# Long-run loads of q and k, one DMA transpose per batch and shared PSUM banks in an attention and channel-mix kernel

## The chip, the cores and the metric

The kernel runs on one core of one Trainium2 chip. The metric is the device time in microseconds (us) of one execution. An execution of the kernel before took 299.62 us (median of three; 299.26 to 300.0). The profile's span is about 1.7 us shorter than the measured time of the same execution. Each execution has a state: slow is one that took over 1.5% longer than the fastest run of the same kernel, the others are fast.

In this text, PE is the matmul engine (TensorE), DVE VectorE, ACT ScalarE, POOL GpSimd, and SP the engine whose queue issues most DMAs. PSUM is the memory that the matmuls write; this program uses eight banks of it, and an instruction of ACT or DVE that reads a result out of a bank is called its evacuation here.

## The reference, cut to what matters

```python
def _attn_ref(q, k, v):                       # (8 batches, 8 heads, 576 positions, 64), fp32
    scores = q @ k^T / 8
    mask_plain = (rel >= 0) & (rel < 32)                      # heads 0..3
    mask_dil   = (rel >= 0) & (rel < 128) & (rel % 4 == 0)    # heads 4..7
    attn = softmax(where(mask, scores, -1e9))
    return attn @ v

def _moe_ref(x, mu_k, mu_r, w_k, w_v, w_r):   # x (8, 576, 512): attention output, heads side by side
    xk = mu_k * x + (1 - mu_k) * x_prev       # x_prev: the position before
    xr = mu_r * x + (1 - mu_r) * x_prev
    k  = relu(xk @ w_k)                       # 512 -> 1024
    v  = k * k @ w_v                          # 1024 -> 512
    return sigmoid(xr @ w_r) * v
```

A batch goes through attention, and its output is mixed into XK and XR (the inputs of the channel mix). The channel mix works in nine tiles of 128 x 4 positions over all eight batches and needs 720 matmuls of 128 x 128 by 512 columns. I call the moment when a batch's XK is complete "that batch's input is ready".

## The kernel before

Every operation is first entered in a list with its engine, an estimated duration, its dependencies and a priority. A small planner then fixes the order on each engine by simulating that list, and the instructions are issued in that order. Each engine, and SP's queue too, then has to take its instructions in the order that was planned, also where an operation comes later than the planner assumed (in e17 below SP stands for 28 us in this way).

```python
pools = {"qk": 2, "st": 7, "v": 2, "kqd": 2, ..., "kr": 2, "K2": 2, "th": 3, "ot": 3, "cm": 4, "pa": 2}
CM = many(4, [128, 512], FP32, "CM", psp)       # channel mix: 4 PSUM banks of its own
PA = many(2, [128, 2, 512], FP32, "PA", psp)    # attention: 2 double banks
def sp_dma(xfer, fn, n=1, **kw):
    return P.op("SP", 0.06 * n, fn, xfer=xfer, **kw)   # planner: a DMA issue takes 0.06 us

def load_qk_cast(b, prio, after=()):            # batches 1..7: POOL issues DMAs that cast fp32 to fp16
    for n_, (part, i) in enumerate(((0, 1), (0, 0), (1, 1), (1, 0))):
        a, e = ((0, 96), (96, 144))[part]       # 96 and 48 partitions, runs of 4 rows (1 KB)
        ... nc.gpsimd.dma_start(out=qk_dst(bq.idx, i, 0, 8, part), in_=qk_src(i, b, 0, 8, a, e))

def pd(i, part, eng):                           # dilated heads: four DMA transposes a batch
    if b > 0:
        ... nc.sync.dma_start_transpose(out=KQD[kqd.idx][:, i, :, p0:p0 + n], in_=...)
        KDR[i, part] = sp_dma(..., tr, dep=[L[1, i, part]], use=[bq, kqd], prio=nxt(0.001))  # 10*b + ...

# channel mix: relu on ACT, square on DVE, tanh on ACT, last product on DVE
nc.scalar.activation(out=KR[kr.idx][:, g], in_=CM[pk.idx], func=AF.Relu, scale=0.5 ** 0.5)
nc.vector.tensor_tensor(out=K2[k2.idx][:, 2 * f2:2 * f2 + 2], in0=KR[kr.idx], in1=KR[kr.idx], op=ALU.mult)
nc.scalar.activation(out=TH[th.idx], in_=CM[pr.idx], func=AF.Tanh, scale=0.5)
nc.vector.scalar_tensor_tensor(out=OT[ot.idx], in0=TH[th.idx], scalar=1.0, in1=CM[pv.idx], op0=ALU.add, op1=ALU.mult)
# ... (cut: v in six windows of 512 packets of 256 B and two dilated parts, scores, softmax, mixing)
```

The softmax here doesn't subtract the row's maximum and nothing guards it: scores larger than these inputs give would overflow.

Of the kernel before, what the change touches and what calls it, by code (L numbers as in the profile page):

```python
# [22 lines left out]
class Op:  # L23
    __slots__ = ("eng", "dur", "fn", "dep", "use", "prio", "lock", "n", "start", "end", "lat", "xfer", "nsucc", "succ", "ready")


class Plan:


    def __init__(self, pools):  # L30
        self.ops = []
        self.pools = pools

    def op(self, eng, dur, fn, dep=(), use=(), prio=0.0, lock=False, lat=None, xfer=None):
        o = Op()
        o.eng, o.dur, o.fn, o.prio, o.lock = eng, dur, fn, prio, lock
        o.dep = [d for d in dep if d is not None]
        o.use = list(use)
        for b in o.use:
            b.left += 1  # L40
        o.lat = {"PE": 0.13, "ACT": 0.08, "DVE": 0.08, "POOL": 0.12, "SP": 0.0}[eng] if lat is None else lat
        o.xfer = xfer
        o.n = len(self.ops)
        o.start = o.end = None
        self.ops.append(o)
        return o

    def run(self, pe_slack=0.12):
        free = {k: [0.0] * n for k, n in self.pools.items()}
        busy = {k: [False] * n for k, n in self.pools.items()}  # L50
        turns = {k: 0 for k in self.pools}
        t_eng = {"PE": 0.0, "ACT": 0.0, "DVE": 0.0, "POOL": 0.0, "SP": 0.0}
        t_dma = 0.0
        dve_lock_end = pool_lock_end = 0.0
        for o in self.ops:
            o.nsucc = len(o.dep)
            o.succ = []
        for o in self.ops:
            for d in o.dep:
                d.succ.append(o)  # L60
        ready = {e: [] for e in t_eng}
        for o in self.ops:
            o.ready = 0.0
            if o.nsucc == 0:
                ready[o.eng].append(o)
# [3 lines left out]
        def slot(b):  # L69
            if b.idx is not None:  # L70
                return 0.0
            fr, bs = free[b.pool], busy[b.pool]
            if b.turn is not None:
                i = b.turn % len(fr)
                return None if bs[i] or turns[b.pool] != b.turn else fr[i]
            c = [fr[i] for i in range(len(fr)) if not bs[i]]
            return min(c) if c else None

        while left:
            best = None  # L80
            for e, lst in ready.items():
                te = t_eng[e]
                be = None
                for o in lst:
                    r = max(te, o.ready)
                    ok = True
                    for b in o.use:
                        s = slot(b)
                        if s is None:
                            ok = False  # L90
                            break
                        r = max(r, s)
                    if not ok:
                        continue
                    if o.lock:
                        r = max(r, pool_lock_end if e == "DVE" else dve_lock_end)
                    k = (r if r > te + 1e-9 else te, o.prio, o.n)
                    if be is None or k < be[0]:
                        be = (k, o)
                if be is not None and (best is None or be[0] < best[0]):  # L100
                    best = be
            assert best is not None, "no operation can start"
            (t, _, _), o = best
            e = o.eng
            ready[e].remove(o)
            for b in o.use:
                if b.idx is None:
                    fr, bs = free[b.pool], busy[b.pool]
                    if b.turn is not None:
                        i = b.turn % len(fr)  # L110
                        turns[b.pool] += 1
                    else:
                        i = min((j for j in range(len(fr)) if not bs[j]), key=lambda j: fr[j])
                    b.idx = i
                    bs[i] = True
            o.start = t
            t_eng[e] = t + o.dur
            o.end = t + o.dur + o.lat
            if o.lock:
                if e == "DVE":  # L120
                    dve_lock_end = t + o.dur
                else:
                    pool_lock_end = t + o.dur
            if o.xfer is not None:
                t_dma = max(t_dma, t + o.dur + 0.6) + o.xfer
                o.end = t_dma + 1.5
            for b in o.use:
                b.left -= 1
                if b.left == 0:
                    free[b.pool][b.idx] = o.end + (0.05 if e != "PE" else 0.0)  # L130
                    busy[b.pool][b.idx] = False
            for s in o.succ:
                s.nsucc -= 1
                sl = pe_slack if s.eng == "PE" and e != "PE" else 0.0
                s.ready = max(s.ready, o.end + sl if s.eng != e else (o.end if o.xfer is not None else t + o.dur))
                if s.nsucc == 0:
                    ready[s.eng].append(s)
# [18 lines left out]
def kernel(  # L156
# [18 lines left out]
    VS = 66  # L175
# [6 lines left out]
    pools = {"qk": 2, "st": 7, "v": 2, "kqd": 2, "qt": 2, "at": 3, "xs": 3, "rc": 4, "xT": 2, "dx": 1,  # L182
             "ring": NR, "kr": 2, "K2": 2, "th": 3, "ot": 3, "cm": 4, "pa": 2}
    P = Plan(pools)
# [4 lines left out]
    QA = many(2, [96, 2, 8, 256], FP16, "QA")  # L189
    QB = many(2, [112, 8, 256], FP16, "QB")  # L190
    ST = many(pools["st"], [128, 1024], FP32, "ST")
    VP = many(2, [128, 6, 4, VS], FP16, "VP")
    VD1 = many(2, [112, 4, 4, VS], FP16, "VD1_")
    VD2 = many(2, [64, 4, 4, VS], FP16, "VD2_")
    KQD = many(2, [128, 2, 8, NP], FP16, "KQD")
    QT = many(2, [128, 2, 4, NP], FP16, "QT")
    KT = many(2, [128, 2, S], FP16, "KT")
# [9 lines left out]
    TH = many(pools["th"], [128, DM], FP32, "TH")  # L207
    OT = many(pools["ot"], [128, DM], FP32, "OT")
# [3 lines left out]
    nmk = const.tile([128, 4], FP32, name="nmk")  # L212
    nmr = const.tile([128, 4], FP32, name="nmr")
# [4 lines left out]
    CM = many(4, [128, 512], FP32, "CM", psp)  # L218
    PA = many(2, [128, 2, 512], FP32, "PA", psp)

    def buf(pool, turn=None):
        return Buf(pool, turn)

# [15 lines left out]
    def setup_mp():  # L239
        nc.vector.tensor_copy(out=MP.rearrange("p (r i) -> p r i", r=4),  # L240
                              in_=M[:, 32:128].rearrange("p (i r) -> p r i", r=4))
# [3 lines left out]
    def setup_m0():  # L245
        for wl in range(2):
            nc.vector.tensor_copy(
                out=M0.rearrange("p (a w h) (r i) -> p w a h r i", a=2, w=2, r=4)[:, wl, 0, 0],
                in_=M[:, 32 * wl:32 * wl + 96].rearrange("p (i r) -> p r i", r=4))
        src = M0.rearrange("p (a w h) c -> p w a h c", a=2, w=2)  # L250
        for wl in range(2):
            for a in range(2):
                for h in range(2):
                    if a or h:
                        nc.vector.tensor_copy(out=src[:, wl, a, h], in_=src[:, wl, 0, 0])

    m0_op = P.op("DVE", 1.6, setup_m0, dep=[mask_op], prio=-8)
# [9 lines left out]
    def setup_zero():  # L267
        for t in AT:
            nc.vector.memset(t, 0.0)
        for t in XT:  # L270
            nc.vector.memset(t[:, :, :, 0:2], 0.0)

    zero_op = P.op("DVE", 1.2, setup_zero, prio=-20)

    def load_mu():
        with nc.allow_non_contiguous_dma(reason="mu"):
            nc.sync.dma_start(out=nmk, in_=moe_mu_k.rearrange("(c p) -> p c", p=128))
            nc.sync.dma_start(out=nmr, in_=moe_mu_r.rearrange("(c p) -> p c", p=128))

    def fix_mu():  # L280
        nc.vector.tensor_scalar(out=nmk, in0=nmk, scalar1=-1.0, scalar2=None, op0=ALU.add)
        nc.vector.tensor_scalar(out=nmr, in0=nmr, scalar1=-1.0, scalar2=None, op0=ALU.add)


    def cast(eng, o, i):
        {"DVE": nc.vector.tensor_copy, "POOL": nc.gpsimd.tensor_copy, "ACT": nc.scalar.copy}[eng](out=o, in_=i)  # L286

    def cast_op(eng, n, o, i, **kw):
        d = {"DVE": dve2(n), "POOL": 0.1 + 0.0009 * n, "ACT": act(n)}[eng]
        return P.op(eng, d, lambda: cast(eng, o(), i()), lock=eng != "ACT", **kw)  # L290

    def sp_dma(xfer, fn, n=1, **kw):
        return P.op("SP", 0.06 * n, fn, xfer=xfer, **kw)

    def pool_dma(xfer, fn, n=1, **kw):
        return P.op("POOL", 0.66 * n, fn, xfer=xfer, **kw)

    W = {}

    def load_w(name, dst, src, eng, prio, cprio=None):  # L300

        s = buf("st")
        shape = dst.shape

        def ld():
            t = ST[s.idx]
            if len(shape) == 3:
                t = t.rearrange("p (a n) -> p a n", a=shape[1])
            nc.sync.dma_start(out=t, in_=src)

        def st():
            t = ST[s.idx]
            return t.rearrange("p (a n) -> p a n", a=shape[1]) if len(shape) == 3 else t

        d = sp_dma(1.35, ld, use=[s], prio=prio)
        W[name] = cast_op(eng, 1024, lambda: dst, st, dep=[d], use=[s], prio=prio if cprio is None else cprio)

    qs = {0: q, 1: k}
    LD = {}

    def qk_src(i, b, h0, h1, a, e):
        return qs[i][b, h0:h1].rearrange("h (p r) d -> p h (r d)", r=4)[a:e]

    def qk_dst(slot, i, h0, h1, part):
        if part == 0:
# [549 lines left out]
```

## Time and profile before

| stretch (us) | what happens | PE busy |
|---|---|---|
| 0 to 39 | weights and batch 0 load; batch 0's input is ready at 39.1 | 17 us |
| 39 to 89 | batch 1; its input is ready only at 89.2 | 31.5 us |
| 89 to 259 | batches 2 to 7, 28.4 us each | 152 of 170 us |
| 259 to 298 | the last two tiles, with no attention left, then the last store | 34.7 us |

From the page of the kernel before: span, busy time of each engine, and the span in 40 slices of 7.5 us, each digit the busy share of a slice in tenths (PEclk is PE's granted clock in tenths).

```profile
span 298.3 us, 5959 instructions
...
PE 234.5 (79%) x2336; PEld 124.9 (42%) x2336; DVE 180.3 (60%) x355; ACT 161.6 (54%) x254; POOL 52.3 (18%) x75
...
PE   1544679922659995699899949997999899599994
...
PEclk9999979975576999599999997999999799999999
DMA  8999999999999999994752792054003102200322
```

PE is the busiest engine, but its ninth and tenth slices are nearly empty, while the DMA engines are full there. The table of stretches puts numbers on this. After the stretch it gives its length, then the busy time of each engine with the count of instructions, PE's granted clock, the mean busy share of the DMA engines (transfers in flight overlap, so it can exceed 1) and GB/s.

```profile
...
core 0: us, PE busy (x) PEld busy (x) DVE busy (x) ACT busy (x) POOL busy (x), PEclk, DMA share, GB/s
60.00:90.00 30.00, 12.85 (x192) 8.60 (x193) 15.89 (x31) 9.64 (x15) 7.15 (x9) 0.61 1.26 209
89.20:259.40 170.20, 151.68 (x1576) 79.31 (x1576) 119.88 (x238) 102.55 (x168) 27.99 (x33) 0.94 0.63 116
```

In the 30 us from 60 to 90 PE worked 12.9 us, and at a clock of 0.61. The Trainium skill ("TensorE: Matmul & The Clock Gate", Part 1) says that an idle array falls to half its clock; the trace agrees: eight matmuls of 512 columns (the product with wv, L795) took 3.55 us at 80.5 us and 1.89 to 1.90 us in the 35 other groups. From 89 to 259 us PE stood still for 18.5 us of 170.

What PE waited for, in the waits view (us in total, times, longest; KQD is the transposed q and k of the dilated heads):

```profile
...
PE CM L752 <- DVE XK L706: 18.1, 8, 4.6
PE PA L568 <- DMA KQD<-QB: 7.2, 1, 7.2
```

SP's own queue in this time, from the timeline (start, duration of the issue, instruction). L372 and L389 load v, L457 is a transpose.

```profile
...
30.07 12.92 SPq L372 DMA_DIRECT2D ST<-in_v_dram  x6
43.09 1.66 SPq L389 DMA_DIRECT2D ST<-in_v_dram  x2
44.85 1.65 SPq L372 DMA_DIRECT2D ST<-in_v_dram  x3
46.60 2.64 SPq L457 DMA_TRANSPOSE KQD<-QA  x1
49.34 4.06 SPq L372 DMA_DIRECT2D ST<-in_v_dram  x3
53.50 2.18 SPq L389 DMA_DIRECT2D ST<-in_v_dram  x1
55.78 5.47 SPq L457 DMA_TRANSPOSE KQD<-QA  x1
61.34 1.21 SPq L457 DMA_TRANSPOSE KQD<-QB  x1
...
63.41 1.21 SPq L457 DMA_TRANSPOSE KQD<-QB  x1
```

The transposes of batch 1 stand between loads of v that belong to later work. Those loads hold SP for long (six issues took 12.9 us), and the last of the four transposes is issued at 63.4 us. The scores of batch 1's dilated heads start at 70.5 us, after PE has waited 7.2 us for it. Two lines of DVE's timeline show when the inputs of batches 1 and 2 became ready (start and duration of the last addition):

```profile
...
87.80 1.36 DVE L706 TENSOR_TENSOR XK<-XK,XT 128x2304 f16<-128x2304 f16 x1
...
122.78 1.36 DVE L706 TENSOR_TENSOR XK<-XK,XT 128x2304 f16<-128x2304 f16 x1
```

### The profile page before, as it was taken

What the parts mean: (1) busy time and instruction counts of PE and PEld (TensorE: products, weight loads), DVE (VectorE), ACT (ScalarE), POOL (GpSimd) and SP (SyncE); (2) the same over time, 40 slices, a digit from 0 to 9 for tenths busy, and PEclk for the clock granted to TensorE, in tenths of its full rate; (3) what the DMA queues carried; (4) which work ended last, traced back from release to release, by engine and by line L of the source; (5) the groups of instructions that cost most, each with busy time, mean ns of one, the idle gap of its engine ahead of it and who ended that gap; (6) DMA issues with size and microseconds to landing.
All of it is one profiled execution on the core that took longest, in us unless ns stands there. A gap on an engine that the chain in (4) does not pass through costs nothing.

```text
span 298.3 us, 5959 instructions
## 1 busy us (share of the span) xinstructions
PE 234.5 (79%) x2336; PEld 124.9 (42%) x2336; DVE 180.3 (60%) x355; ACT 161.6 (54%) x254; POOL 52.3 (18%) x75
## 2 busy tenths in 40 slices
PE   1544679922659995699899949997999899599994
PEld 0433334421424554445455424453554355244441
DVE  4555653633764756796886638749767876833221
ACT  2518988423246735865775375638665672566220
POOL 2224008106113225232031401020000000000000
PEclk9999979975576999599999997999999799999999
DMA  8999999999999999994752792054003102200322
GB/s 168 203 224 365 306 221 210 161 158 201 261 226 171 220 193 248 203 193 77 168 150 41 117 249 82 0 108 115 2 2 105 37 1 73 70 0 2 91 96 94
DMA packets 76187, 41.87 MB, mean 140 GB/s; under 512 B 45440, under 2 KB 69504, under 8 KB 76160
## 3 DMA queue, kind: packets, MB, share of 16 engines
q1 hardware_dynamic: 59584, 33.24, 50.0%
q0 software_dynamic: 16576, 8.26, 22.9%
q8 instruction: 18, 0.29, 0.4%
q14 instruction: 9, 0.07, 0.1%
HBM read 36.18 MB, written 9.44 MB: 153 GB/s over the span
## 4 chain that ended last, share of the span: by engine, by line
PE 63%; DVE 17%; DMA 11%; SPq 5%; ACT 2%; issue 1%; POOL 0%; DVEq 0%; ACTq 0%; POOLq 0%
PE CM L752 24%; PE CM L795 18%; PE CM L788 9%; DVE XK L706 3%; DMA ST<-in_moe_w_k_dram 3%; DVE XK L698 3%; PE PA L433 3%; DMA out_dram<-OT 3%; DMA KQD<-QB 2%; DMA ST<-in_k_dram 2%; SPq L457 2%; DVE OT L799 2%; DVE XS L493 2%; PE PA L540 2%; PE PA L589 2%
## 5 line engine op out<-in xcount | busy, mean ns | idle before, releaser
L752 PE MATMUL CM<-XK,wk 128*128 128x512 f16 x288 | 77.8, 414 | 18.2 <-DVE XK L706 18.1
L795 PE MATMUL CM<-wv,K 128*128 128x512 f16 x288 | 69.9, 387 | 0.0
L756 ACT ACTIVATE KR<-CM 128x512 f16<-128x512 f32 x72 | 42.9, 598 | 30.6 <-PE CM L752 30.1
L799 DVE SCALAR_TENSOR_TENSOR OT<-TH,CM 128x512 f32<-128x512 f32 x36 | 24.7, 687 | 39.6 <-PE CM L795 33.2
L752 PEld LDWEIGHTS <-wk 128*128 128x128 f16 x288 | 27.2, 103 | 48.6 <-issue 25.9
L765 DVE TENSOR_TENSOR K<-KR 128x1024 f16<-128x1024 f16 x36 | 27.7, 770 | 23.6 <-ACT KR L756 23.5
L795 PEld LDWEIGHTS <-K 128*128 128x128 f16 x288 | 26.7, 99 | 30.2 <-issue 1.7
L788 PE MATMUL CM<-wr,XR 128*128 128x512 f16 x144 | 36.4, 380 | 0.0
L791 ACT ACTIVATE TH<-CM 128x512 f32<-128x512 f32 x36 | 21.4, 596 | 24.6 <-PE CM L788 21.0
L493 DVE TENSOR_TENSOR XS<-PA,RC 96x512 f16<-96x512 f32 (+2 forms) x48 | 30.9, 644 | 1.7 <-DVE RC L489 0.2
L521 ACT ACTIVATE AT<-PA 128x768 f16<-128x768 f32 x24 | 19.0, 807 | 14.4 <-PE PA L517 14.4
L702 ACT ACTIVATE XR<-DX,nmr 128x576 f16<-128x576 f16 (+2 forms) x36 | 23.2, 714 | 2.4 <-DVE DX L695 2.4
L579 DVE TENSOR_TENSOR AT<-AT,M 112x896 f16<-112x896 f16 x16 | 13.0, 815 | 15.8 <-ACT AT L573 15.8
L286 POOL CAST VP<-ST 128x768 f16<-128x768 f32 (+1 forms) x15 | 13.5, 904 | 50.5 <-DMA ST<-in_v_dram 26.2
L286 POOL CAST VD<-ST 112x1024 f16<-112x1024 f32 (+1 forms) x15 | 15.5, 1048 | 28.9 <-PE PA L589 22.2
L573 ACT ACTIVATE AT<-PA 112x896 f16<-112x896 f32 x16 | 14.4, 914 | 9.0 <-PE PA L568 8.9
L445 ACT ACTIVATE KT<-PA 128x768 f16<-128x768 f16 (+1 forms) x16 | 10.4, 652 | 15.8 <-PE PA L433 15.7
L788 PEld LDWEIGHTS <-XR 128*128 128x128 f16 x144 | 12.8, 98 | 13.4 <-issue 0.5
L433 PE MATMUL PA<-ident,QA 96*64 96x96 f16 x256 | 10.7, 241 | 8.0 <-DVE QA L286 5.5
L605 ACT ACTIVATE XT<-PA 128x448 f16<-128x448 f16 x16 | 8.7, 542 | 14.7 <-PE PA L601 14.6
L568 PE MATMUL PA<-KQD 64*112 64x112 f16 x128 | 7.1, 247 | 9.1 <-DMA KQD<-QB 7.2
L540 PE MATMUL PA<-VP,AT 128*128 128x65 f16 x192 | 10.8, 205 | 4.2 <-ACT KQD L477 2.8
(73 smaller groups left out, 259.8 us busy)
## 6 DMA issues: line engine op xcount, KB each, us to landing
ST<-in_v_dram SPq DMA_DIRECT2D x48, 128.0 KB, 6.5
ST<-in_v_dram SPq DMA_DIRECT2D x8, 448.0 KB, 6.9
QA<-in_k_dram POOLq DMA_DIRECT2D x7, 384.0 KB, 8.4
QA<-in_q_dram POOLq DMA_DIRECT2D x7, 384.0 KB, 9.4
ST<-in_v_dram SPq DMA_DIRECT2D x8, 256.0 KB, 6.8
ST<-in_moe_w_k_dram SPq DMA_DIRECT2D x4, 512.0 KB, 9.1
ST<-in_moe_w_v_dram SPq DMA_DIRECT2D x4, 512.0 KB, 10.9
out_dram<-OT SPq DMA_DIRECT2D x8, 256.0 KB, 5.3
```

What stands on the lines that cost most here:

```text
L286: {"DVE": nc.vector.tensor_copy, "POOL": nc.gpsimd.tensor_copy, "ACT": nc.scalar.copy}[eng](out=o, in_=i)
L433: nc.tensor.transpose(out=t[64 * e:64 * e + 64, hp * 4 + r], in_=src_qk(i, part, 2 * hp + e, 64 * r), identity=idn(i, part), tile_position ...
L493: nc.vector.tensor_tensor(out=XS[xs.idx][0:n, 0:g].rearrange("p w (h d) -> p w h d", h=4), in0=fin(po)[0:n, :, :, 0:64], in1=RC[rc.idx][0: ...
L521: nc.scalar.activation(out=AT[at.idx][:, :, 0:96].rearrange("p (a g) c -> p a g c", a=2), in_=PA[ps.idx][:, :, 0:384].rearrange("p a (g c) ...
L702: nc.scalar.activation(out=XR[:, c, :, a:a + n], in_=DX[0][:, c, :, o:o + n], func=AF.Copy, scale=nmr[:, c:c + 1])
L752: nc.tensor.matmul(out=o, lhsT=wk[:, c, f * 128:f * 128 + 128], rhs=XK[:, c, :, a0:a0 + 128], start=(c == 0), stop=(c == 3))
L756: nc.scalar.activation(out=KR[kr.idx][:, g], in_=CM[pk.idx], func=AF.Relu, scale=0.5 ** 0.5)
L765: nc.vector.tensor_tensor(out=K2[k2.idx][:, 2 * f2:2 * f2 + 2], in0=KR[kr.idx], in1=KR[kr.idx], op=ALU.mult)
L788: nc.tensor.matmul(out=CM[pr.idx], lhsT=XR[:, c, r, a:a + 128], rhs=wr[:, c], start=(c == 0), stop=(c == 3))
L791: nc.scalar.activation(out=TH[th.idx], in_=CM[pr.idx], func=AF.Tanh, scale=0.5)
L795: nc.tensor.matmul(out=CM[pv.idx], lhsT=K2[k2.idx][:, f, 128 * r:128 * r + 128], rhs=wv[:, f], start=(f == 0), stop=(f == NF - 1))
L799: nc.vector.scalar_tensor_tensor(out=OT[ot.idx], in0=TH[th.idx], scalar=1.0, in1=CM[pv.idx], op0=ALU.add, op1=ALU.mult)
```

## The change

Its intent: load q and k of the plain heads in runs of 2304 B over all 128 partitions and of the dilated heads in rows of 1 KB, without a casting DMA; cast on POOL (batch 0 and 1: on any free engine); turn the dilated q and k of a batch in one DMA transpose that is planned right after their load; let attention and channel mix share PSUM banks (from batch 1 on they overlap in banks 4 and 5), for which all eight banks become four tiles PA of two banks each; and let the planner choose between DVE and ACT for some copies and scalings. The planner itself got other costs.

```diff
-pools = {..., "cm": 4, "pa": 2}
-CM = many(4, [128, 512], FP32, "CM", psp)         # before: each bank of the channel mix is a tile of its own
-PA = many(2, [128, 2, 512], FP32, "PA", psp)
+PA = many(4, [128, 2, 512], FP32, "PA", psp)      # after: two banks in each tile
+P = Plan(pools, {"pa": OPTIONS["pa"], "p1": OPTIONS["p1"], "cm": OPTIONS["cm"], ...})
+OPTIONS = dict(..., split=1, pa=[(0, 1), (2, 3), (4, 5)], p1=[(0,), (1,), (2,), (3,)],
+               cm=[(4,), (5,), (6,), (7,)], ..., p=0, v=0, xe=0, sk=('DVE','ACT'), sr=('DVE','ACT'),
+               ep='P', ed='P', er='P', ev='P', ew='P', st=5, b1=dict(ep='*', ed='*', ..., ew='P'))
-    return P.op("SP", 0.06 * n, fn, xfer=xfer, **kw)
+    return P.op("SP", t or 0.47 * n, fn, xfer=xfer, **kw)
+def load_plain_qk(b, prio, cprio, engs):
+    for n_, (i, t) in enumerate(((1, k), (0, q))):
+        src = t[b, 0:4].rearrange("(g e) (x y) d -> (e x) g (y d)", g=2, x=64)     # runs of 9 rows
+        LD[b]["p", i] = piece(1.65, 1152, ..., src, lambda i=i: QP[bq.idx][:, i], engs[n_], ...)
         if b > 0:
             def tr():
-                nc.sync.dma_start_transpose(out=KQD[kqd.idx][:, i, :, p0:p0 + n], in_=...)
-            KDR[i, part] = sp_dma(..., tr, dep=[L[1, i, part]], use=[bq, kqd], prio=nxt(0.001))
+                nc.sync.dma_start_transpose(out=KQD[...].rearrange("p a (g x) -> p (a g) x", x=128),
+                                            in_=QD[bq.idx].rearrange("p a g x -> p (a g x)"))
+            KDR.append(sp_dma(..., tr, t=OPT["ttr"], dep=list(parts_), use=[bq, kqd], prio=-90 + 10 * b + 0.15))
+    W["wr"] = P.op("POOL", 0.7, lambda: nc.gpsimd.dma_start(out=wr, in_=wrr), ...)   # wr, wv: casting DMA
# ... (cut: v of the plain heads in two DMAs of the same 256 B runs, masks, planner internals)
```

## The prediction

> **What bounds the kernel now.** The page gives PE 234.5 of 298.3 us busy. The table of stretches shows where the other 64 us lie: PE was busy 7.2 of the first 20 us, 10.4 of 20 to 40, and only 12.9 of 60 to 90 (granted clock 0.61 there), i.e. 49 of the first 90 us. From 122.8 to 259.5 us PE was busy 122.7 of 136.7 us (five batches, 27.3 us each), and the last 34.7 us are PE alone. So before about 120 us DMA feeds too slowly (mean DMA share 1.03 to 1.34); after it PE is the limit with 10% gaps.
>
> The stall at 60 to 90 us is read in the timeline: batch 1's four transposes of the dilated q and k were issued at 46.6, 55.8, 61.3 and 63.4 us, one queue entry held SP for 5.5 us, and they stood between v loads of which each 512-packet window held SP about 1.1 us. The scores of the dilated heads waited 7.2 us for the last one (waits view), batch 1's channel-mix input was ready at 89.2 us and batch 2's at 124 us.
>
> **What the change removes, adds, moves.**
> - DMA packets: q/k of a batch go from 2304 cast packets of 1 KB (queue 0: 22.9% of 16 engines over 16,576 packets, about 66 ns each) to 512 long runs plus 1152 runs of 1 KB without a cast. v keeps its 256 B packets. Four transposes a batch become one, planned early. Estimate: DMA time per batch falls by only 10 to 20%, but the queue order and SP's blocking improve more.
> - POOL: casts grow. One costs about 1.04 us per 1024 columns (lines view); q, k and v of a batch are about 8200 columns, so about 8.5 us a batch, some 65 us in all, against 29 us now. The Trainium skill (SBUF — State Buffer, "SBUF: two separate sides") says that the pair of ports shared by GpSimd and VectorE is locked for a whole instruction. The trace agrees: one mask multiply on DVE (L579, median 0.62 us) took 3.48 us beside POOL casts at 72 us. This eats a part of the gain.
> - PSUM: attention gets three double banks and shares eight; this trims the 10% gaps, by perhaps 2 to 6 us.
> - PE work stays nearly equal: 720 large matmuls, floor 0.216 us each (0.865 us per four in the chain), 156 us; the attention's about 45 us.
>
> **On the critical path.** Estimate: batch 1's channel-mix input comes at about 60 instead of 89 us and batch 2's at about 88 instead of 124. Then five periods of about 26.5 us to the last batch, its first channel-mix matmul at about 221 instead of 259.5, and 35 to 37 us to the end: about 257 us.
>
> **Prediction: 257 us**, eight times in ten between 243 and 275. Faster by over 2%: 0.94; within 2%: 0.04; slower: 0.02.
>
> **What would show it.** Right: PE over 85% of the span; first channel-mix matmul of batch 1 before 65 us; one transpose issue per batch; last batch's tail still about 35 us; packets 10 to 20% fewer; POOL busy 60 us or more. Wrong: the same stall at 60 to 90 us, with SP still blocked by v loads, or periods over 28 us with PE waiting for DVE while POOL casts.
>
> **What would make it wrong.** DVE stretched by POOL's casts in the steady state (slower, 270 and more); a first stage that is much shorter because long runs move faster (245 or less); a single transpose that lands late because it now needs all casts of a batch.

## The result and the profile after

The changed kernel took 276.77 us (median of four; fast runs 275.05, 276.28 and 277.26, one slow run of 279.64; the median of the fast ones alone is 276.28), against 299.81 us for the kernel before. The ratio of the two is 0.92 (interval 0.913 to 0.927). Ratios here are the mean time of one kernel's fast runs over that of the other's of the same rounds, so not quite the ratio of the medians that are quoted. So the kernel is 8% faster, but the prediction of 257 us (243 to 275) is 20 us too low and its range just misses.

The same lines of the page, kernel after (slices of 6.8 us):

```profile
span 273.3 us, 6031 instructions
...
PE 226.9 (83%) x2388; PEld 122.5 (45%) x2388; DVE 185.8 (68%) x377; ACT 155.0 (57%) x260; POOL 69.3 (25%) x85
...
PE   1564986899998599899998879988886889999992
...
PEclk9995599599999989999999999999999999999999
DMA  7999999989999999999998995940021012110331
```

The hole at 60 to 90 us is gone. The same table of stretches, the second one again from batch 1's input to batch 7's:

```profile
...
60.00:90.00 30.00, 28.19 (x316) 14.99 (x316) 22.35 (x42) 18.23 (x33) 12.90 (x14) 1.00 1.06 234
63.40:231.40 168.00, 146.80 (x1618) 78.78 (x1617) 127.87 (x260) 102.13 (x176) 52.25 (x52) 0.99 0.72 174
```

From 60 to 90 us PE now works 28.2 us in place of 12.9, at full clock. But from batch 1's input to batch 7's the kernel needs 168.0 us where it needed 170.2, and PE's idle time there is 21.2 us (168.0 less 146.8) where it was 18.5. For the five periods from batch 2's to batch 7's input alone, the kernel before and then the kernel after:

```profile
...
124.14:259.43 135.29, 122.63 (x1226) 62.91 (x1226) 97.43 (x199) 81.94 (x136) 15.40 (x17) 0.96 0.44 92
...
94.50:231.42 136.92, 120.04 (x1314) 64.27 (x1314) 103.50 (x215) 83.08 (x143) 39.63 (x40) 0.99 0.65 161
```

SP's queue and the two inputs, in the timeline:

```profile
...
31.55 2.65 SPq L366 DMA_DIRECT2D ST<-in_v_dram  x2
38.67 5.88 SPq L494 DMA_TRANSPOSE KQD<-QD  x1
44.60 0.56 SPq L366 DMA_DIRECT2D ST<-in_k_dram  x1
```

```profile
...
62.65 0.76 DVE L724 TENSOR_TENSOR XK<-XK,XT 128x1152 f16<-128x1152 f16 x1
...
93.03 1.47 DVE L724 TENSOR_TENSOR XK<-XK,XT 128x1152 f16<-128x1152 f16 x1
```

Batch 1's transpose (L494) is issued at 38.7 us, before any load of batch 2, and batch 1's input is ready at 63.4 in place of 89.2 us. That is 26 us, slightly more than the whole gain. What PE waits for has changed too, in the waits view:

```profile
...
PE PA L780 <- ACT KR L784: 5.4, 13, 0.8
PE PA L780 <- DVE XK L724: 5.0, 3, 2.6
PE PA L830 <- ACT TH L826: 2.9, 5, 1.2
...
PE PA L780 <- ACT TH L826: 2.4, 2, 1.7
...
PE PA L823 <- DVE OT L834: 0.8, 2, 0.4
...
PE PA L596 <- DMA KQD<-QD: 0.3, 1, 0.3
```

The view's largest line, 6.0 us for batch 0's q and k (QP) in the first 20 us, is left out; the kernel before waits 5.5 us there. PE no longer waits long for XK (it did for 18.1 us). New are waits for the relu (KR), the tanh (TH) and the last product (OT), which free PSUM banks: in the whole run they sum to 13.6 us, all such lines of the view added. The kernel before has none.

### The profile page after: what moved, and what is told of

Its sections match the earlier page's. It is cut to its first block, busy times and chain, and to the rows that moved or that the text cites. A ratio compares the mean times of both kernels' runs of the same rounds, so it can differ in the third digit from the quotient of the medians.

```text
span 273.3 us, 6031 instructions
## 1 busy us (share of the span) xinstructions
PE 226.9 (83%) x2388; PEld 122.5 (45%) x2388; DVE 185.8 (68%) x377; ACT 155.0 (57%) x260; POOL 69.3 (25%) x85
## 2 busy tenths in 40 slices
DMA packets 68732, 48.49 MB, mean 177 GB/s; under 512 B 43096, under 2 KB 59488, under 8 KB 68704
## 4 chain that ended last, share of the span: by engine, by line
PE 53%; DVE 16%; ACT 13%; DMA 11%; issue 6%; SPq 1%; POOL 0%; ACTq 0%; DVEq 0%; POOLq 0%
PE PA L830 18%; PE PA L780 17%; PE PA L823 9%; DMA ST<-in_q_dram 5%; ACT KR L784 4%; DVE OT L834 3%; DMA KQD<-QD 3%; ACT TH L826 3%; DMA ST<-in_moe_w_k_dram 2%; PE PA L481 2%; DVE K L794 2%; DVE XS L524 2%; DVE XT L338 1%; DVE AT L558 1%; ACT XT L334 1%
## 5 line engine op out<-in xcount | busy, mean ns | idle before, releaser
L780 PE MATMUL PA<-XK,wk 128*128 128x512 f16 x288 | 72.4, 397 | 13.2 <-ACT KR L784 5.4
L830 PE MATMUL PA<-wv,K 128*128 128x512 f16 x288 | 69.7, 386 | 3.6 <-ACT TH L826 2.9
L784 ACT ACTIVATE KR<-PA 128x512 f16<-128x512 f32 x72 | 40.5, 596 | 40.2 <-PE PA L780 29.2
L834 DVE SCALAR_TENSOR_TENSOR OT<-TH,PA 128x512 f32<-128x512 f32 x36 | 24.7, 685 | 36.1 <-ACT TH L826 15.7
L823 PE MATMUL PA<-wr,XR 128*128 128x512 f16 x144 | 36.8, 379 | 2.6 <-DVE OT L834 0.8
L826 ACT ACTIVATE TH<-PA 128x512 f32<-128x512 f32 x36 | 21.3, 598 | 30.2 <-PE PA L830 21.2
L336 POOL CAST QD<-ST 128x1024 f16<-128x1024 f32 (+1 forms) x19 | 17.5, 930 | 30.8 <-DMA ST<-in_k_dram 14.8
L336 POOL CAST QP<-ST 128x1152 f16<-128x1152 f32 x12 | 15.1, 1262 | 16.0 <-DMA ST<-in_k_dram 8.9
L724 DVE TENSOR_TENSOR XK<-XK,XT 128x1152 f16<-128x1152 f16 (+2 forms) x18 | 14.0, 787 | 4.2 <-ACT XK L718 3.8
L718 ACT ACTIVATE XR<-DX,nm 128x576 f16<-128x576 f16 (+2 forms) x21 | 15.0, 736 | 0.0
```

What stands on the lines that cost most here:

```text
L336: nc.gpsimd.tensor_copy(out=o, in_=i)
L780: nc.tensor.matmul(out=o, lhsT=wk[:, c, f * 128:f * 128 + 128], rhs=XK[:, c, :, a0:a0 + 128], start=(c == 0), stop=(c == 3))
L784: nc.scalar.activation(out=KR[kr.idx][:, g0:g0 + G], in_=view(), func=AF.Relu, scale=0.5 ** 0.5)
L823: nc.tensor.matmul(out=view(pr)[:, g], lhsT=XR[:, c, rr[g], a:a + 128], rhs=wr[:, c], start=(c == 0), stop=(c == 3))
L826: nc.scalar.activation(out=TH[th.idx][:, 0:m], in_=view(pr), func=AF.Tanh, scale=0.5)
L830: nc.tensor.matmul(out=view(pv)[:, g], lhsT=K2[k2.idx][:, f, 128 * rr[g]:128 * rr[g] + 128], rhs=wv[:, f], start=(f == 0), stop=(f == NF - 1))
```

## The experiments

Labels beginning with e are runs; those on the changed kernel are compared with its 276.8 us, those on the kernel before with 299.8 us. "Input ready" is read from DVE's timeline.

### 1. Three rival causes of the missing 20 us: banks, DMA packets, POOL's casts

**e1**: give the channel mix its four banks back.

```diff
-pa=[(0, 1), (2, 3), (4, 5)]
+pa=[(0, 1), (2, 3)]
```

> The changed kernel with the attention's third double bank (4,5) taken away, so the channel mix has banks 4 to 7 to itself as before the change. Theory P (sharing the banks makes PE wait for evacuations): PE's waits for ACT KR, ACT TH and DVE OT in the steady state, 12.5 us between batch 1's and batch 7's input, fall under 4 us, and the time falls by 6 to 12 us to 265 to 271 us. Rival (the sharing pays or does not matter): within 1% of 276.8 us or slower, and waits for XK or for attention results take the place.

Measured: 275.13 us, ratio to the kernel before 0.921 (0.912 to 0.930), so the same as with shared banks. PE's waits for KR, TH and OT halved, from 13.6 to 6.8 us, but waits on the attention (AT, the weights of the softmax, and XT, the attention output turned) came in their place, as these lines of its waits view show; the path from batch 1's to batch 7's input took 169.9 us.

```profile
...
PE PA L569 <- DVE AT L558: 3.4, 6, 0.9
PE PA L780 <- ACT KR L784: 2.9, 7, 0.5
PE PA L547 <- DVE XT L338: 2.2, 1, 2.2
```

Between batch 1's and batch 7's input these waits fell from 12.5 to 6.6 us, not under 4, and the time fits the rival. Sharing banks 4 and 5 neither earned the 2 to 6 us that the prediction gave it nor cost anything. e1 leaves two banks in each tile; part 2 comes back to this.

**e2**: the same bytes of v in long runs (wrong result).

```diff
-in_=bass.AP(v.tensor, a.offset, [[D, 128], [96 * D, 23], [1, D]])
+in_=bass.AP(v.tensor, v[b, 0].offset, [[23 * D, 128], [D, 23], [1, D]])
```

> Wrong result on purpose: the plain heads' v is fetched in 128 long runs of 5.9 KB a batch in place of 2944 runs of 256 B; bytes, instructions and their order stay the same. Theory D (loads still set the pace after the change): batch 1's input comes 3 us earlier or more, later periods shorten, 265 us or less. Rival (the pace is set on PE, ACT and DVE): within 1.5%, 273 to 278 us, with the DMA share falling to about 0.8 in 60 to 150 us.

Measured: 276.09 us, batch 1's input at 64.1 us; packets fell from 68,732 to 46,204, the DMA share over the first 180 us only from 1.01 to 0.94, and the time did not move. The Trainium skill ("DMA: Bandwidth & Descriptors", Why small descriptors are slow) warns of a fixed cost per packet; here 2,800 packets of 256 B less per batch did not shorten the run, since the loads are not what the steady state waits for.

**e3**: from batch 2 on, POOL copies 8 columns of each row group only (wrong result).

```diff
+    if CUT and engs == ("POOL",):       # CUT is set from batch 2 on
+        return P.op(engs[0], costs(n, engs)[engs[0]], lambda: copy(engs[0], cut(o()), cut(i())), **kw)
```

> Wrong result on purpose: from batch 2 on every cast on POOL copies 8 columns of each row group in place of all; order and waits stay the same. Theory C (POOL's casts lengthen DVE through the shared ports and so the periods): 260 to 268 us, and DVE busy falls by 5 us or more. Rival (the casts lie beside the critical path): within 1.5% of 276.8 us, DVE busy falls by 2 to 4 us only.

Measured: 273.81 us (three fast runs of 271.4 to 274.6 us, one slow), ratio 0.914 (0.900 to 0.927), not to be told from the changed kernel's 0.92 (0.913 to 0.927). The busy line of its page:

```profile
...
PE 224.9 (82%) x2388; PEld 122.0 (45%) x2388; DVE 174.2 (64%) x377; ACT 155.1 (57%) x260; POOL 28.7 (11%) x85
```

With POOL at 28.7 in place of 69.3 us, DVE fell from 185.8 to 174.2 us although it did the same work. So the casts do lengthen DVE's instructions, by 11.6 us in all, in agreement with the Trainium skill ("SBUF — State Buffer", SBUF: two separate sides: the pair of ports shared by GpSimd and VectorE is locked for a whole instruction). But most of this lies beside the critical path: the mean of the fast runs is 3 us lower, and even that is within the intervals.

### 2. Which engines hold PE in the steady state

**e5**: from the fourth tile on, relu, square, tanh and last product work on 64 of 512 columns (wrong result; the order of all engines stays).

```diff
+Z = 512 if i < 3 else 64
-nc.scalar.activation(out=KR[kr.idx][:, g0:g0 + G], in_=view(), func=AF.Relu, ...)
+nc.scalar.activation(out=KR[kr.idx][:, g0:g0 + G, 0:Z], in_=view()[:, :, 0:Z], func=AF.Relu, ...)
# the square, the tanh and the last product likewise
```

> Wrong result on purpose: from the fourth channel-mix tile on, relu, square, tanh and the last product work on 64 of 512 columns; matmuls, order and waits stay. Theory E (PE's 21 us of gaps between batch 1's and batch 7's input come from in-order ACT and DVE holding PSUM banks and attention work): PE idle there falls below 12 us and the time to 262 us or less. Rival W (PE's own work, more than the prediction summed, fills the periods): within 2% of 276.8 us.

Measured: 262.96 us. The stretch from batch 1's to batch 7's input, in the table of stretches:

```profile
...
63.90:219.30 155.40, 144.84 (x1618) 77.84 (x1617) 114.62 (x260) 85.82 (x176) 51.19 (x52) 0.99 0.78 188
```

It is 155.4 us, and PE idles for 10.6 us of it in place of 21.2. From batch 3's input on its idle time is 0.7 to 1.0 us a batch, where the changed kernel has 2.7 to 4.0. So theory E holds in its direction, and 262.96 us is just above its forecast of 262: what ACT and DVE do for the channel mix sets PE's gaps. 263 us is also close to what was predicted for the real kernel.

**e6**: the 480 large matmuls of tiles 4 to 9 with 256 columns; the evacuations read those 256 twice, so keep their size (wrong result).

```diff
+Z = 128 if i < 3 else 64
-nc.tensor.matmul(out=o, lhsT=wk[...], rhs=XK[:, c, :, a0:a0 + 128], ...)
+nc.tensor.matmul(out=o[...4 * Z columns...], lhsT=wk[...], rhs=XK[:, c, :, a0:a0 + Z], ...)
# XR @ wr and K @ wv likewise
```

> Wrong result on purpose: from the fourth tile on the 480 large matmuls have 256 columns in place of 512, about 51 us less PE work at 0.107 us each; evacuations keep their size. If PE's work alone fills the periods (W), the time falls by 40 us or more to 236 us or less. If ACT, DVE and their order set the pace (E), it falls by under 20 us, to 257 us or more.

Measured: 244.95 us, 32 us less for 51 us less PE work: between the two forecasts. PE idles more (33.0 us on that stretch, which took 151.0 us). PE's work is a large part of the pace and ACT and DVE are close behind it; no single engine is "the" limit.

**e10**: as e5, but on DVE only (square and last product; relu and tanh full).

```diff
-nc.vector.tensor_tensor(out=K2[...][:, 2 * f2:2 * f2 + 2], in0=KR[kr.idx], in1=KR[kr.idx], op=ALU.mult)
+nc.vector.tensor_tensor(out=K2[...][:, 2 * f2:2 * f2 + 2, 0:Z], in0=KR[kr.idx][:, :, 0:Z], ...)
# the last product likewise
```

> Wrong result on purpose: the changed kernel with only DVE's square and last product on 64 of 512 columns from the fourth tile on, ACT's relu and tanh full. If DVE is what holds PE, most of the 14 us of the run with all four short are kept, 267 us or less; if ACT is, 272 us or more.

Measured: 270.66 us, between the two forecasts. DVE's part gives 6 of the 14 us; the other 8 come only when ACT's part is shortened too. (By the ratios to the kernel before in the same rounds, 0.907 and 0.878 against 0.92, it is some 4 of 13 us.)

**e9**: e5's edit on the kernel before (wrong result).

```diff
-nc.scalar.activation(out=KR[kr.idx][:, g], in_=CM[pk.idx], func=AF.Relu, ...)
+nc.scalar.activation(out=KR[kr.idx][:, g, 0:Z], in_=CM[pk.idx][:, 0:Z], func=AF.Relu, ...)
# the square, the tanh and the last product likewise
```

> Wrong result on purpose: the kernel before with the same shortening of relu, square, tanh and last product as in the run on the changed kernel that gave 263 us. If the evacuations bind only after the change (a limit that the change uncovered), the kernel before loses under 2%, 294 us or more. If they bound before too, it falls by 10 to 15 us, to 285 to 290 us.

Measured: fast runs of 294.1 to 297.7 us, ratio 0.989 (0.980 to 0.998), about 3 us; one execution, the profiled one, was slow (401 us, clock 0.60), so its trace is not used. The same shortening is worth 14 us after the change and 3 us before it. The evacuations hardly bound before; after the change they do.

A count made from both traces shows the same from the other side. I paired each relu, tanh and last product with the matmuls that it reads, in the program's order, over the stretch from batch 1's to batch 7's input, and took the time from the end of those matmuls to its start:

| mean lag behind its matmuls, us | kernel before | kernel after |
|---|---|---|
| relu (KR) | 0.11 | 0.53 |
| tanh (TH) | 0.10 | 0.67 |
| last product (OT) | 0.54 | 0.56 |

In the kernel before ACT nearly always stood ready. In the kernel after, a bank stays taken for 1.12 us after a relu's matmuls in place of 0.71. ACT is no busier in this stretch (102.1 us of 168.0 against 102.6 of 170.2), so it is its order and what it waits for, not its load, that differ.

What it waits for can be read in the timeline. Eight matmuls, four for each of two relus, and the two relus, in the kernel before:

```profile
...
97.78 1.89 PE L752 MATMUL CM<-XK,wk 128*128 128x512 f16 x8
...
98.84 0.60 ACT L756 ACTIVATE KR<-CM 128x512 f16<-128x512 f32 x1
...
99.77 0.60 ACT L756 ACTIVATE KR<-CM 128x512 f16<-128x512 f32 x1 [0.33 <-PE CM L752]
```

and in the kernel after:

```profile
...
126.02 1.89 PE L780 MATMUL PA<-XK,wk 128*128 128x512 f16 x8 [0.35 <-ACT KR L784]
...
127.94 1.08 ACT L784 ACTIVATE KR<-PA 128x512 f16<-128x512 f32 x2 [1.17 <-PE PA L780]
```

Before, the first relu starts at 98.84 us, when half of the matmuls are done (the brackets give the idle time before and who ended it). After, both start only when all eight are done, at 127.9 us: the trace has no signal (no semaphore update, for which ACT could wait) at the end of the first relu's own four matmuls. In the stretch this is so for 13 of 48 relus and 5 of 23 tanhs, which start 1.1 and 1.8 us behind their own matmuls (the others 0.31 and 0.35 us); in the kernel before, and in e8, for none.

The plan of the changed kernel was printed with the bank of each operation. In all 18 cases matmuls for the other bank of the same two-bank tile are planned between the evacuation and its own matmuls; in the 51 cases where none are, no signal is missing. The other way round, of PE's 13.6 us of waits for KR, TH and OT, 11.5 us (23 of 27) are, as the profile puts them down, for the evacuation of the other bank of the tile that PE is about to write. So this program orders its work by tile, and two banks in one tile wait for each other. What that costs in time no run tests, since every variant of the changed kernel has the same tiles; e1 lost half of these waits, and its time stayed the same within the intervals.

### 3. Which part of the change brought the gain

**e7**: the transpose as four, at the same place.

```diff
+for g0, g1 in ((0, 5), (5, 9), (9, 14), (14, 18)):
+    nc.sync.dma_start_transpose(out=KQD[...][:, g0:g1], in_=QD[...][:, 128 * g0:128 * g1])
```

> The single DMA transpose of a batch's dilated q and k is issued as four transposes of 4 or 5 blocks, at the same place in the same order. If one transpose in place of four is what took the 60 to 90 us stall away, batch 1's input comes 5 us later or more and the time rises by over 2%. If the place in the queue and the plain loads did it, within 1% of 276.8 us.

Measured: 277.02 us over all four runs, two of them slow; the two fast ones took 272.79 and 276.56 us, ratio 0.917 (0.907 to 0.926); batch 1's input at 63.7 us in a profile of a slow execution. One transpose or four makes no difference that these runs show.

**e16**: the transpose with its old priority, all else as changed.

```diff
-dep=list(parts_), use=[bq, kqd], prio=-90 + 10 * b + 0.15)
+dep=list(parts_), use=[bq, kqd], prio=nxt(0.001))
```

> The DMA transpose gets its old priority, so that on the SP queue it stands behind the next batch's loads. If its place removed the stall, batch 1's input comes at 75 us or later and the time is 288 us or more; if the plain loads and the packets did, batch 1's input stays below 68 us and the time within 2% of 276.8 us.

Measured: 300.14 us (the kernel before, in its two fast runs of the same rounds: 295.31 and 299.5): the whole gain is gone. SP's queue in the timeline, PE's largest wait, and the stretch from 60 to 90 us:

```profile
...
63.03 0.59 SPq L421 DMA_DIRECT2D SV<-in_v_dram  x1
63.67 5.64 SPq L418 DMA_DIRECT2D SV<-in_v_dram  x1
69.35 6.70 SPq L494 DMA_TRANSPOSE KQD<-QD  x2
```

```profile
...
PE PA L596 <- DMA KQD<-QD: 9.9, 2, 7.9
```

```profile
...
60.00:90.00 30.00, 14.09 (x244) 10.68 (x245) 15.16 (x30) 10.83 (x17) 14.78 (x15) 0.55 1.07 240
```

The transpose of batch 1 (with that of batch 2) is issued at 69.4 us behind the loads of batches 2 and 3, batch 1's input is ready at 90.5 us, and PE works 14.1 of the 30 us, at a clock of 0.55. The planner reordered PE, DVE and ACT too, so this is not a change of SP's order alone, but the chain is visible step by step.

**e4**: from batch 2 on, q and k of the plain heads and their v by casting DMA again.

```diff
-p=0, v=0, xe=0
+p=1, v=1, xe=0
```

> One part undone: from batch 2 on q and k of the plain heads and their v are cast by DMA again, from POOL's queue, in place of a plain load and a POOL cast. If the gain came from taking the casts out of DMA, the time rises to 285 us or more and waits for loaded data come back; if it came from the order of the transposes and the queue, the time stays within 2% of 276.8 us. Batch 1 is loaded as in the changed kernel, so its input should be ready at about 63 us in both cases.

Measured: two fast runs of 282.9 and 286.0 us, two slow ones of 288.9 and 290.9; ratio 0.952 (0.932 to 0.972), against 0.92. Batch 1's input came at 61.9 us, but batch 3's at 132.9 in place of 120.5 us, and POOL waited for loads of dilated q and k for 70 us (29.6 us in the changed kernel). The loads without a cast, of the plain heads from batch 2 on, are worth some 3%.

**e15**: casting DMA for batch 1 alone.

```diff
-b1=dict(p=0, v=0, ep='*', ...)
+b1=dict(p=1, v=1, ep='*', ...)
```

> Only batch 1's plain q, k and v are loaded by casting DMA again. If the plain loads are what brought batch 1's input from 89 to 63 us, it comes at 70 us or later and the time rises by 5 us or more; if the order is, it stays at 61 to 66 us and the time within 1.5% of 276.8 us.

Measured: 282.65 us; batch 1's input at 67.9 us, between the two forecasts. Batch 0's input came 4 us later already (34.3 in place of 30.2 us), as the casting DMAs load the same DMA engines. So batch 1's loads without a cast, for the plain heads and their v, carry 4 to 5 us of its 26, while the place of the transpose alone moves it by 27 (e16). Neither e4 nor e15 gives the dilated q and k, on which the transpose waits, back to a casting DMA. Only e17 has them so, together with all else of the kernel before.

**e8**: the kernel before with the new planner alone (0.47 us for an issue, and so on).

```diff
-class Plan: ...        # and 0.06 us for a DMA issue on SP
+class Plan: ...        # the changed kernel's, and 0.47 us
```

> The kernel before with the new scheduling code alone: 0.47 us for a DMA issue in place of 0.06, 1.9 us to land in place of 1.5, and a slow clock after idling. If the new order is what paid, 285 us or less; if the loads and layouts did, within 2% of 299.8 us, with the stall at 60 to 90 us still there.

Measured: 302.55 us, ratio 1.012 (1.005 to 1.018), batch 1's input at 91.6 us. The planner's costs alone bring nothing.

**e17**: e8 with the four transposes given the early priority.

```diff
-use=[bq, kqd], prio=nxt(0.001))
+use=[bq, kqd], prio=-90 + 10 * b + 0.15)
```

> The kernel before with the new scheduling code (302.6 us by itself) and with its four transposes a batch given the new, early priority, so that on the SP queue they stand before the batch's v loads. If the early place alone carries the gain, batch 1's input comes at 75 us or earlier and the time is 287 us or less. If it needs the plain loads too, because the old casting DMAs land late and SP then waits in front of the v loads, 295 us or more.

Measured: 310.91 us, ratio 1.036 (1.029 to 1.043), so slower by 3.6%. Batch 1's input does come earlier, at 77.3 us, but now SP stands in front of the transposes until the casting DMAs have landed, and the loads of v stand behind it. SP's waits in front of transposes (L487; the view's other large lines, left out, are output stores that wait for their data, such as 80.3 us for OT; the kernel before has 63.3 us of these):

```profile
...
SPq L487 <- DMA QA<-in_q_dram: 16.7, 4, 6.4
...
SPq L487 <- DMA QA<-in_k_dram: 6.2, 2, 5.4
SPq L487 <- DMA QB<-in_k_dram: 5.3, 1, 5.3
```

That is 28 us of standing. The Trainium skill ("DMA: Bandwidth & Descriptors", Anatomy of one DMA, which describes DMAs issued by POOL) says that "any semaphore wait happens on the issuing sequencer before dispatch". This trace agrees for SP: it stands before the transpose, and the DMAs behind it are issued later. How much of the 311 us this costs stays open, for PE's order differs as well: from 102.7 to 145.0 us PE was busy for 27.2 us at a granted clock of 0.50, and after batch 7's input 65.8 us were left to do, where the kernel before has 38.9. So an early place did not pay with the old loads, and did with the new ones; that the casting DMAs' late landing is the reason is argued, not shown.

### 4. Tries at a better version

**e11**: the copies of the transposed attention output on ACT alone.

```diff
-xe=0
+xe=1
```

> A try at a better version: the copies of the transposed attention output go to ACT alone (from batch 1 on), which takes some 7 us from DVE. If DVE's load is the limit, 268 to 273 us; if it is the order as a whole, within 1% of 276.8 us.

**e12**: e11, and the planner reckons 0.4 us in place of 0.12 from ACT or DVE to PE.

```diff
-order = P.run()
+order = P.run(pe_slack=0.4)
```

> A try at a better version: as the copies on ACT, and the plan reckons 0.4 us in place of 0.12 between ACT or DVE and PE, so PE's fixed order leans less on results that are due just in time. If PE's gaps come from a fixed order that is planned too tightly, the idle time of PE from batch 1 to 7 falls by 5 us or more and the time to 270 us or less; if not, 273 to 278 us.

**e13**: four buffers of KR and TH in place of two (TH and OT cut to the one row in use, to fit).

```diff
-pools=dict(at=4)
+pools=dict(at=4, kr=4, th=4)
```

> KR and TH in four buffers in place of two (TH and OT cut to the one row that is used). If the two KR buffers hold ACT's relus back until DVE has squared, PE's waits for KR, TH and OT (13.6 us in the changed kernel) fall by half and the time to 268 to 272 us; if not, within 1% of 276.8 us.

**e14**: e13, and the copies of the plain q and k may go to DVE in every batch.

```diff
-QTR[i, hp] = flex(576, ("ACT", "DVE") if b == 0 else ("ACT",), ...)
+QTR[i, hp] = flex(576, ("ACT", "DVE"), ...)
```

> As with four KR buffers, and the copies of the transposed plain q and k may go to DVE too in every batch (19 us of ACT in the changed kernel). If ACT's queue is what lags, relus start earlier after their matmuls (mean 0.53 us in the changed kernel) and the time is 266 to 271 us; if both engines are equally tight, within 1% of 276.8 us.

**e18**: XK scaled on DVE alone and XR on ACT alone.

```diff
-sk=('DVE','ACT'), sr=('DVE','ACT')
+sk=('DVE',), sr=('ACT',)
```

> The changed kernel with the scaling of XK on DVE alone and of XR on ACT alone, as before the change. If the free choice of engine costs time by the fixed order that follows from it, 268 to 273 us; if it does not matter, within 1% of 276.8 us; if it pays, 280 us or more.

Measured, in this order: 282.99, 280.98, 282.42, 284.39 and 282.27 us. All five are correct and all are slower than the changed kernel, by 1.5 to 2.8% (ratios to the kernel before: e11 0.948, e12 0.942, e18 0.939, against 0.92). In e13 PE's waits for KR, TH and OT rose from 13.6 to 18.6 us, in e12 to 19.5, in e14 to 16.1; so neither two KR buffers nor a tight plan is the cause by itself. Each small edit gives a new order on all engines beside what it changes itself, and the times scatter over some 3%, no less than the effects that were sought. How much of this is order alone was not separated; e12 against e11, where only the plan differs, is 2 us. None beats the changed kernel; e1's 275.1 us is not to be told from it.

## Why the prediction was wrong

- **The cause of the gain was right.** The prediction read the stall at 60 to 90 us as transposes stuck on SP's queue, and put batch 1's input at about 60 in place of 89 us. It came at 63.4 us. e16 shows that the place of the transpose carries it, e7 that their number does not, e4 and e15 that the plain heads' loads without a cast add a few per cent, and e17 that the early place alone, with the old loads, does not pay.
- **The step that failed: "this trims the 10% gaps, by perhaps 2 to 6 us" and "five periods of about 26.5 us".** From batch 2's to batch 7's input five periods took 136.9 us (27.4 each), as in the kernel before (135.3 us), and PE's gaps there grew from 12.7 to 16.9 us. What the runs showed in its place: once the feed no longer held PE, the channel mix's own evacuations did. e5 takes 14 us away, 3 us in the kernel before (e9). That attention uses banks 4 and 5 too is not the means (e1); of the 13.6 us of new waits, 11.5 us are for the other bank of a two-bank tile, into which the change had put the channel mix's banks. I had taken PE's gaps of before for waits that would vanish; they were replaced by others.
- **The sum of the miss**, in the profiled run (273.3 us against 257): batch 1's input 3.4 us late; batch 2's period 31.1 us in place of 28, 3.1 us; the five periods, some 4 us; from batch 7's input to the end 41.9 us where the prediction has "35 to 37 us to the end", about 6 us and the largest single term. Of the last term, 3 us are an error of reading: in the kernel before this part took 38.9 us, and I counted only PE's 34.7 and left the last product and its store out. 10 more matmuls (170 in place of 160), 2.2 us at 0.216, were left for it too. The profiled run was also the fastest: the median is 1.7 us above it, and the span leaves out another 1.7 us of each execution.
- **POOL's casts: right in the mechanism, wrong in weight.** POOL was busy for 69.3 us (forecast: 60 or more), and the casts lengthen DVE by 11.6 us; but "this eats a part of the gain" is not shown: e3 moved the time by 1%, within its interval.
- **What was to show it**: one transpose a batch (seven, as said), batch 1's first channel-mix matmul before 65 us (its input was ready at 63.4 us and groups of these matmuls run from then on), packets 10 to 20% fewer (9.8%, just missed), PE over 85% of the span (83%, wrong), a tail of about 35 us (41.9, wrong). Of its signs of being wrong, two of the five periods did take over 28 us (31.2 and 30.3), but e3, with POOL's casts cut short, left them at 31.4 and 29.5 us, so those casts are not the reason.
- **The range** was too narrow for a change that alters the order on every engine: in the tries of part 4 small edits, each with a new order, moved the time by up to 3%, or 8 us.

What stays open: what the late start of the relus and tanhs behind their matmuls costs. Not ACT's load, not two KR buffers and not banks 4 and 5 make it; the tiles of two banks make a good part of it, as the signals in the trace and the plan show. The rest, the fixed order of three engines that are all at 57 to 83%, is argued and not shown. The changed kernel with one tile for each bank of the channel mix would test it.

## What to carry to other kernels

Where an in-order queue issues the DMAs, ask for each wait on the critical path what stands in front of it there; moving one transpose in front of the next batch's loads was worth 23 us, while fewer packets, one transpose in place of four, and shared PSUM banks were worth nothing measurable. An early place can also hurt: in e17, with sources that landed late, SP stood before its transposes for 28 us and the kernel took 311 us. Two banks that are to be filled and read in turn should not lie in one tile without a look at who then waits for whom. And when a feed stall goes, don't count the remaining gaps of the busiest engine as gain: shorten the next engines on purpose, with a wrong result, to see how close they are.

## What the Trainium skill lacked or had wrong

- "DMA: Bandwidth & Descriptors", Issuing engines are not separate DMA queues, calls the time that a sequencer takes to initiate a DMA "usually small relative to the DMA itself". Here one transpose of 18 blocks held SP for 3.3 to 7.0 us (median 5.9), with a median of 6.9 us from issue to landing, and six loads of 512 packets of 256 B held it for 12.9 us while the DMA engines were full. Everything behind in that queue is issued later by as much.
- No page says that the place of a DMA transpose in its issuing queue can decide a kernel's time: 300.1 us late, 276.8 us early.
- "DMA: Bandwidth & Descriptors", Why small descriptors are slow, gives a cost per packet; e2 shows that taking a third of all packets away (68,732 to 46,204) can leave the time as it was (276.1 us), with the DMA share of the first 180 us going only from 1.01 to 0.94. A full DMA share was no proof that DMA sets the pace.
